# State products on half tiles of the array with one query plane, and the inverse of the running decays as one wide reciprocal in place of a backward scan

## The chip, the cores and the metric

The kernel runs on one core of one Trainium2 chip. The metric is the device time of one execution in microseconds (us). The core has a matrix engine (TensorE, PE in the profile, with its weight loads as PEld), three engines for elementwise work (VectorE or DVE, ScalarE or ACT, GpSimd or POOL), and SyncE (SP), which issues the transfers. Each engine works through its own instructions in order.

## The reference

A gated linear attention, followed by two feed-forward layers:

```python
# B, H, S, D = 4, 8, 768, 48; one 48 x 48 state for each batch and head
for t in range(S):
    state = alpha[:, :, t, :, None] * state + np.einsum('bhd,bhe->bhde', k[:, :, t], v[:, :, t])
    y[:, :, t] = np.einsum('bhd,bhde->bhe', q[:, :, t], state)
x = y.transpose(0, 2, 1, 3).reshape(3072, 384)
h = x @ w_in                      # 384 x 2048
x = (h * np.cos(h)) @ w_out       # 2048 x 384
out = ((x @ w_a) * (x @ w_b)) @ w_out2   # 384 x 1536, 1536 x 384
```

All arrays are float32, and alpha lies between 0.8 and 1.

## The kernel before

**The attention** is cut into 48 units: unit u is one batch and one chunk of 64 steps, with its 8 heads laid out as 4 pairs. The even head of a pair stands on partitions 64 to 111, the odd one on 0 to 47 (`HEADS`). For each unit the kernel does the following.

- *Front* (`plan_front`). DVE scans the running product of the decays `a` (L303, 112 x 260: 4 pairs of 65 columns, column 0 of each is 1). It then needs the inverse `r = 1/a`: a reciprocal of the last column of each pair (L312, 112 x 4, into `last`), and a scan from the right (L315, 112 x 260) that multiplies this by the decays step by step. POOL writes `m = q * a` (L327, for each head of the pair an instruction of its own, 48 x 256), and `k * r` is made by DVE for the first eight units and by POOL for the others (L340). ACT sums the squares of `a` and `r` (L344); this sum decides at the end whether the numbers were in range.
- *Scores* (`plan_scores`). PE multiplies the scaled keys with the scaled queries (L374) and transposes the keys (L383); ACT copies the transposed keys to SBUF (L389, `kn`), and DVE masks the scores into plane 0 of `m` (L407, or L413 from unit 16 on).
- *Back* (`plan_back`). PE makes the new state (L444, and L450 to add the old one) and the outputs: scores times values (L461), and, for units below `APART` = 16 that have a predecessor, the old state `s` times the scaled queries (L466). There are 14 such units. In L466 a product has 112 rows: the tile `m` has three planes, and planes 1 and 2 hold the queries of one head each, with zeros on the rows of the other head. ACT and DVE move the outputs to the tile `x_t` (L505, L508), and DVE multiplies the new state by the last decay (L535).

From unit 16 on the state is put beside the values, so that L461 alone makes the outputs.

**The layers.** A step of layer 1 is a block of 9 matrix products on `hp` (L656), then round, fraction, sine, product and a split in two parts that ACT and DVE take in turns (L706, L709, L714, L717, L721, L725), then 9 products into `acc_t` (L663). There are 96 such steps. Sixteen weight tiles for it are decoded on the way (ACT L599, L604 and L625, DVE L610 and L616, POOL L636), from transfers into `st_t`. Layer 2 follows.

**What sets the order.** `Plan` is a list scheduler that runs when the kernel is built. Each operation has an engine, a planned time in us, what it comes after, and at times a due time; the order that it finds is what each engine gets. An operation with `port=True` is not planned beside another one with that flag, be it on DVE or on POOL. The planned times are numbers in the code: 0.18 for the reciprocal L312 and 0.7 for the scan L315.

Of the kernel before, what the change touches and what calls it, by code (L numbers as in the profile page):

```python
# [10 lines left out]
F32 = mybir.dt.float32  # L11
# [6 lines left out]
ALU = mybir.AluOpType  # L18

B, H, S, D = 4, 8, 768, 48  # L20
# [4 lines left out]
C = 64  # L25
NCH = S // C
NU = B * NCH
NP = H // 2
P = 128
KT = DM // P  # L30
# [9 lines left out]
NE4 = NP * D  # L40
# [16 lines left out]
APART = 16  # L57
NLATE = NPAIR2 - NPAIR1
DVE_DECAY = 0
ACT_LOW = 16  # L60
# [106 lines left out]
def chunked(ctx: ExitStack, tc: tile.TileContext, u_in: bass.AP, wts: bass.AP, out: bass.AP, in_range: bass.AP):  # L167
# [18 lines left out]
    first = att.tile([112, NP, SEP], F32, name="first", bufs=1)  # L186
    last = att.tile([112, NP, SEP], F32, name="last", bufs=1)
    nc.vector.memset(first, 0.0)
    nc.vector.memset(last, 0.0)
    nc.vector.memset(first[:, :, 0:1], 1.0)  # L190
    mask = att.tile([P, 1, 1, C], F32, name="mask", bufs=1)
    nc.gpsimd.memset(mask, 1.0)
    for r0 in (0, 64):
# [3 lines left out]
        )  # L197
    m_t = [att.tile([P, 3, NP, C], F32, name=f"m{i}", bufs=1) for i in range(3)]
    for i, t in enumerate(m_t):
        (nc.gpsimd if i else nc.vector).memset(t[:, 1:3], 0.0)  # L200
    s_t = [att.tile([112, NE4], F32, name=f"s{i}", bufs=1) for i in range(2)]
# [54 lines left out]
    def part(u, i):  # L256
        return un[u]["in"][0:112, NA + i * NC4:NA + (i + 1) * NC4].rearrange("p (c t) -> p c t", t=C)
# [16 lines left out]
    def plan_load(u):  # L274
        d, ops = un[u], U[u]
        if "ld" in ops:
            return ops["ld"]
        def load():
            if u < UG:
                t = wpool.tile([P, 2, 2 * DM], F32R, name="w_t").bitcast(F32)  # L280
                d["in"] = t.rearrange("p a c -> p (a c)")[:, 0:IN_COLS]
            else:
                d["in"] = att.tile([P, IN_COLS], F32, name="in_t", bufs=NIN)
            cols = W_A + 2 * NE4 if u < APART else IN_COLS
            cuts = (0, NA + 1, cols) if u == 0 else (0, cols)
            for c0, c1 in zip(cuts, cuts[1:]):
                nc.sync.dma_start(out=d["in"][:, c0:c1], in_=u_in[u, :, c0:c1])

        ops["ld"] = op(SP, 1.5, load, lag=1.7)
        ops["in_last"] = take("w_t", NPAIR1, ops["ld"]) if u < UG else take("in", NIN, ops["ld"])  # L290
        return ops["ld"]

    def plan_front(u):
# [17 lines left out]
        def recip():  # L311
            nc.vector.reciprocal(last[:, :, C:SEP], d["a"][:, :, C:SEP])  # L312

        def scan_r():
            nc.vector.tensor_tensor_scan(  # L315
                d["r"].rearrange("p c t -> p (c t)")[:, ::-1], d["in"][0:112, NA:0:-1],
                last.rearrange("p c t -> p (c t)")[:, ::-1], 0.0, op0=ALU.mult, op1=ALU.add,
            )

        rc = op(DVE, 0.18, recip, [sa, U[u - 1]["sr"] if u else None])  # L320
        sr = ops["sr"] = op(DVE, 0.7, scan_r, [rc], port=True)
        m = m_t[u % 3]
# [4 lines left out]
                lambda rows=rows, i=i: nc.gpsimd.tensor_tensor(  # L327
                    m[rows, i + apart], part(u, 0)[rows], d["a"][rows, :, 1:], op=ALU.mult
                ),
                [sa, *m_before], port=True,  # L330
            )
            for rows, i in HEADS
        ]
# [28 lines left out]
    def plan_scores(u, block=None):  # L362
# [7 lines left out]
        def score():  # L370
            for c in range(2):
                for b in range(2):
                    for rows, h in HEADS:
                        nc.tensor.matmul(  # L374
                            sc_t[rows_of(b, h), b, c, :], kt[rows, 2 * b + c, :],
                            m[rows, h + apart, 2 * b + c, :], start=True, stop=True,
                        )
# [44 lines left out]
    def plan_back(u):  # L422
# [32 lines left out]
        def outputs():  # L455
            for p in range(NP):
                b, c = divmod(p, 2)
                for h, r0, n in ((0, 0, C), (1, 64, D)):
                    w = d["in"][:, W_A + h * NE4 + p * D:W_A + h * NE4 + p * D + n]
                    k_rows = P if apart or h else 112  # L460
                    nc.tensor.matmul(  # L461
                        ys_t[r0:r0 + n, b, c, :], w[0:k_rows], m[0:k_rows, 0 if apart else h, p, :],
                        start=True, stop=not carry,
                    )
                    if carry:
                        nc.tensor.matmul(  # L466
                            ys_t[r0:r0 + D, b, c, :], s_t[u % 2][:, p * D:p * D + D], m[0:112, h + 1, p, :],
                            start=False, stop=True,
                        )
            if u < UG:  # L470
                keep_warm(1)
# [10 lines left out]
        else:  # L482
# [10 lines left out]

            us = ou = op(PE, 1.75 + (1.0 if carry else 0.0), block, [kn, ld, *mk, *ma, *before], due=due)
        ops["us_op"] = [us]
# [439 lines left out]
def step_by_step(  # L935
# [76 lines left out]
    with tc.For_i(0, NG, 1) as g:  # L1012
        cols = bass.ds(g * G, G)
        x = pool.tile([P, KT, G], F32, name="g_x", bufs=1)
        for j in range(KT):
            for r0, f0, n in (
                (0, 2 * j * D, D), (48, 6 * D + j, 16), (64, (2 * j + 1) * D, D), (112, 7 * D + j, 16)
            ):
                step = KT if n == 16 else 1
                nc.sync.dma_start(out=x[r0:r0 + n, j, :], in_=y_all[f0:f0 + (n - 1) * step + 1:step, cols])  # L1020
# [115 lines left out]
```

## Time and profile before

| | us |
|---|---|
| median of 3 runs (lowest, highest) | 976.39 (975.45, 978.84) |
| profiled execution | 973.26 |
| its span in the trace | 971.4 |
| PE busy in the span | 939.9 |
| DVE busy | 540.5 |
| ACT busy | 403.2 |
| POOL busy | 226.5 |

The span of the trace is 1.9 us shorter than the profiled execution's own time. The page cuts the span into 40 slices of 24.3 us and shows a tenth of busy time with each digit; the attention fills the first 18 slices, beside layer 1. A windows table gives the same in us for stretches that one chooses. In a timeline the first number is the start, the second the duration, and brackets give the idle time of the engine before the instruction and what ended it.

### The profile page before, as it was taken

How to read it: one execution, taken by the hardware profiler on the slowest of the kernel's cores; microseconds unless marked ns; L12 is line 12 of the kernel's file. 1: busy time of each engine (PE TensorE's matmuls, PEld its weight loads, DVE VectorE, ACT ScalarE, POOL GpSimd, SP SyncE). 2: the span in 40 equal slices, each digit the busy share in tenths (PEclk: the TensorE clock that was granted, in tenths of full speed). 3: DMA queues.
4: the chain of work that ended last, by engine and by line, in shares of the span. 5: the costliest groups of instructions: out<-in, count | busy, mean ns of one | idle time of the engine just before them, and what ended most of it. 6: DMA issues, size and time to landing. Idle time of an engine off the chain costs nothing.

```text
span 971.4 us, 16849 instructions
## 1 busy us (share of the span) xinstructions
PE 939.9 (97%) x6935; PEld 766.3 (79%) x6935; DVE 540.5 (56%) x951; ACT 403.2 (42%) x754; POOL 226.5 (23%) x259
## 2 busy tenths in 40 slices
PE   6798989999999999999999999999999999999996
PEld 4677768888888888888887888888888888888884
DVE  7899998767777786776777842222222222222221
ACT  3477755545545455446665523112113113112111
POOL 4556543313322232312224321001001001000000
PEclk8999999999999999999999999999999999999998
DMA  9355412212221221203223400000000000000000
GB/s 369 106 199 184 164 38 78 90 62 81 88 63 54 89 89 54 64 1 139 98 98 112 149 0 33 1 1 33 1 0 33 1 1 33 0 1 33 1 1 36
DMA packets 17700, 64.96 MB, mean 67 GB/s; under 512 B 2384, under 2 KB 4816, under 8 KB 17616
## 3 DMA queue, kind: packets, MB, share of 16 engines
q1 hardware_dynamic: 17616, 63.81, 19.0%
q8 instruction: 56, 0.92, 0.4%
q14 instruction: 28, 0.23, 0.1%
HBM read 56.72 MB, written 4.72 MB: 63 GB/s over the span
## 4 chain that ended last, share of the span: by engine, by line
PE 87%; DVE 6%; DMA 2%; ACT 2%; issue 1%; POOL 1%; SPq 0%; ACTq 0%
PE acc_t L663 33%; PE hp L656 18%; PE xy L656 15%; PE ap L656 15%; PE xy L461 2%; DMA st_t<-wts 2%; PE xy L374 1%; DVE wf_t L610 1%; DVE wf_t L616 1%; DMA w_t<-u_in 1%; PE xy L383 1%; DVE c_t L709 1%; DVE ar_t L303 1%; PE xy L444 1%; DVE glo_t L725 1%
## 5 line engine op out<-in xcount | busy, mean ns | idle before, releaser
L663 PE MATMUL acc_t<-ghi_t,w_t 128*128 128x512 f32 x972 | 301.1, 391 | 1.0 <-ACT ghi_t L721 1.0
L656 PE MATMUL hp<-x_t,w_t 128*128 128x512 f32 (+1 forms) x882 | 216.4, 390 | 3.2 <-DMA x_t<-x_t 3.2
L663 PEld LDWEIGHTS acc_t<-ghi_t,w_t 128*128 128x128 f32 x972 | 181.6, 188 | 39.3 <-ACT ghi_t L721 1.9
L663 PE MATMUL acc_t<-glo_t,w_t 128*128 128x512 f32 x486 | 190.1, 391 | 3.8 <-DVE glo_t L725 3.8
L822 DVE TENSOR_TENSOR xy<-c_t,xy 128x512 f32<-128x512 f32 x72 | 50.1, 696 | 258.0 <-PE xy L656 257.9
L656 PEld LDWEIGHTS hp<-x_t,w_t 128*128 128x128 f32 x882 | 161.1, 188 | 36.8 <-ACT w_t L625 3.3
L656 PE MATMUL xy<-x_t,w_t 128*128 128x512 f32 x594 | 145.6, 390 | 0.0
L656 PE MATMUL ap<-x_t,w_t 128*128 128x512 f32 x540 | 132.2, 389 | 0.0
L656 PEld LDWEIGHTS xy<-x_t,w_t 128*128 128x128 f32 x594 | 111.5, 188 | 23.4
L656 PEld LDWEIGHTS ap<-x_t,w_t 128*128 128x128 f32 x540 | 101.4, 188 | 21.1
L819 ACT COPY c_t<-ap 128x512 f32<-128x512 f32 x72 | 42.3, 587 | 167.9 <-PE ap L656 167.8
L663 PEld LDWEIGHTS acc_t<-glo_t,w_t 128*128 128x128 f32 x486 | 91.2, 188 | 25.6 <-DVE glo_t L725 6.4
L826 ACT CAST ghi_t<-xy 128x512 fp32r<-128x512 f32 x72 | 42.2, 586 | 138.3 <-DVE xy L822 138.3
L706 ACT ACTIVATE c_t<-hp 128x512 int32<-128x512 f32 x96 | 57.5, 599 | 67.4 <-PE hp L656 67.1
L636 POOL TENSOR_TENSOR w_t<-wf_t,w_t 128x768 fp32r<-128x768 f32 x32 | 64.0, 1999 | 92.1 <-ACT w_t L625 92.1
L781 POOL TENSOR_TENSOR x_t<-x,x_t 128x512 fp32r<-128x512 f32 x18 | 23.7, 1343 | 251.0 <-ACT x_t L778 251.0
L714 ACT ACTIVATE c_t<-c_t 128x512 f32<-128x512 f32 x96 | 60.6, 631 | 46.7 <-DVE c_t L709 45.9
L709 DVE CUSTOM_DVE_ANT_0 c_t<-c_t,hp 128x512 f32<-128x512 int32 x96 | 65.6, 683 | 25.6 <-ACT c_t L706 24.7
L721 ACT CAST ghi_t<-hp 128x512 fp32r<-128x512 f32 x96 | 56.4, 587 | 54.1 <-DVE hp L717 53.5
L717 DVE TENSOR_TENSOR hp<-c_t,hp 128x512 f32<-128x512 f32 x96 | 65.8, 685 | 19.7 <-ACT c_t L714 19.2
L830 DVE TENSOR_TENSOR glo_t<-xy,ghi_t 128x512 fp32r<-128x512 f32 x72 | 49.8, 692 | 47.3 <-ACT ghi_t L826 47.3
L725 DVE TENSOR_TENSOR glo_t<-hp,ghi_t 128x512 fp32r<-128x512 f32 x96 | 65.7, 684 | 17.1 <-ACT ghi_t L721 16.3
(100 smaller groups left out, 923.3 us busy)
## 6 DMA issues: line engine op xcount, KB each, us to landing
st_t<-wts SPq DMA_DIRECT2D x34, 768.0 KB, 4.3
in_t<-u_in SPq DMA_DIRECT2D x32, 626.0 KB, 3.8
in_t<-u_in SPq DMA_DIRECT2D x8, 578.0 KB, 9.5
out<-o_t SPq DMA_DIRECT2D x18, 256.0 KB, 2.1
w_t<-u_in SPq DMA_DIRECT2D x7, 578.0 KB, 7.8
x_t<-x_t SPq DMA_DIRECT2D x48, 48.0 KB, 2.9
w_t<-u_in SPq DMA_DIRECT2D x1, 447.5 KB, 3.5
w_t<-u_in SPq DMA_DIRECT2D x1, 130.5 KB, 2.2
```

What stands on the lines that cost most here:

```text
L636: nc.gpsimd.tensor_tensor(t[:, 1], conv.pop(i), t[:, 0].bitcast(F32), op=ALU.subtract)
L656: nc.tensor.matmul(acc, wt[:, w, j * P:(j + 1) * P], r[:, j, :], start=i == 0, stop=i == len(terms) - 1)
L663: nc.tensor.matmul(accs[j], wt[:, w, j * P:(j + 1) * P], r, start=first and i == 0, stop=last and i == 2)
L706: nc.scalar.activation(s["c"].bitcast(I32), s["u"], AF.Identity, bias=-0.25, scale=-1.0)
L709: nc.vector._custom_dve(TENSOR_ADD_SAT, out=s["c"], in0=s["c"].bitcast(I32), in1=s["u"], s0=0.25, s1=-0.75)
L714: nc.scalar.activation(s["c"], s["c"], AF.Sin, bias=math.pi / 2, scale=TWO_PI)
L717: nc.vector.tensor_tensor(s["u"], s["c"], s["u"], op=ALU.mult)
L721: nc.scalar.copy(s["hi"], s["u"])
L725: nc.vector.tensor_tensor(s["lo"], s["u"], s["hi"].bitcast(F32), op=ALU.subtract)
L819: nc.scalar.copy(s["c"], s["a"])
L822: nc.vector.tensor_tensor(s["b"], s["c"], s["b"], op=ALU.mult)
L830: nc.vector.tensor_tensor(s["lo"], s["b"], s["hi"].bitcast(F32), op=ALU.subtract)
```

## The change

- `r` is now one reciprocal of all of `a`, 112 x 260 (planned time 0.42, no `port`). The backward scan, the tile `last` and its clearing are gone.
- `m` has two planes for all units. For units below 16 plane 1 holds the queries of both heads, written by one POOL instruction of 112 x 256 where there were two of 48 x 256. The clearing of planes 1 and 2 (one instruction on DVE, two on POOL) is gone.
- The product of the old state with the queries takes 48 rows for each head, at partitions 64 and 0, and writes to either half of the output's partitions. The eight of them stand behind the eight products of scores and values, not between them.
- For this the two heads of the second bank (pairs 2 and 3) change places in the outputs, so the rows of `w_in` and the slices of the fallback path are permuted (`LOW`, `HIGH`).
- A load for a unit below 16 has 16 more columns, 1172 for 1156.
- The planned time of a block of PE work from unit 8 on is 1.5 us, and 0.85 more with an old state (1.75 and 1.0 before).

```diff
+LOW, HIGH = (0, 2, 5, 7), (1, 3, 4, 6)
...
-    last = att.tile([112, NP, SEP], F32, name="last", bufs=1)
     nc.vector.memset(first, 0.0)
-    nc.vector.memset(last, 0.0)
...
-    m_t = [att.tile([P, 3, NP, C], F32, name=f"m{i}", bufs=1) for i in range(3)]
-    for i, t in enumerate(m_t):
-        (nc.gpsimd if i else nc.vector).memset(t[:, 1:3], 0.0)
+    m_t = [att.tile([P, 2, NP, C], F32, name=f"m{i}", bufs=1) for i in range(3)]
...
-            cols = W_A + 2 * NE4 if u < APART else IN_COLS
+            cols = W_A + 2 * NE4 + C - D if u < APART else IN_COLS
...
         def recip():
-            nc.vector.reciprocal(last[:, :, C:SEP], d["a"][:, :, C:SEP])
-
-        def scan_r():
-            nc.vector.tensor_tensor_scan(
-                d["r"].rearrange("p c t -> p (c t)")[:, ::-1], d["in"][0:112, NA:0:-1],
-                last.rearrange("p c t -> p (c t)")[:, ::-1], 0.0, op0=ALU.mult, op1=ALU.add,
-            )
-
-        rc = op(DVE, 0.18, recip, [sa, U[u - 1]["sr"] if u else None])
-        sr = ops["sr"] = op(DVE, 0.7, scan_r, [rc], port=True)
+            nc.vector.reciprocal(d["r"], d["a"])
+
+        sr = op(DVE, 0.42, recip, [sa])
...
-                    m[rows, i + apart], part(u, 0)[rows], d["a"][rows, :, 1:], op=ALU.mult
+                    m[rows, i], part(u, 0)[rows], d["a"][rows, :, 1:], op=ALU.mult
...
-            for rows, i in HEADS
+            for rows, i in (((slice(0, 112), 1),) if apart else HEADS)
...
-                            m[rows, h + apart, 2 * b + c, :], start=True, stop=True,
+                            m[rows, 1 if apart else h, 2 * b + c, :], start=True, stop=True,
...
-                for h, r0, n in ((0, 0, C), (1, 64, D)):
+                for h in range(2):
+                    rows = rows_of(b, h)
+                    n = D if rows.start else C
...
-                        ys_t[r0:r0 + n, b, c, :], w[0:k_rows], m[0:k_rows, 0 if apart else h, p, :],
-                        start=True, stop=not carry,
+                        ys_t[rows.start:rows.start + n, b, c, :], w[0:k_rows], m[0:k_rows, 0 if apart else h, p, :],
+                        start=not carry or c == 0, stop=not carry,
                     )
-                    if carry:
-                        nc.tensor.matmul(
-                            ys_t[r0:r0 + D, b, c, :], s_t[u % 2][:, p * D:p * D + D], m[0:112, h + 1, p, :],
-                            start=False, stop=True,
-                        )
+            if carry:
+                for c in range(2):
+                    for b in range(2):
+                        for rows, h in HEADS:
+                            p, r0 = 2 * b + c, rows_of(b, h).start
+                            nc.tensor.matmul(
+                                ys_t[r0:r0 + D, b, c, :], s_t[u % 2][rows, p * D:p * D + D], m[rows, 1, p, :],
+                                start=False, stop=c == 1,
+                            )
...
-            us = ou = op(PE, 1.75 + (1.0 if carry else 0.0), block, [kn, ld, *mk, *ma, *before], due=due)
+            us = ou = op(PE, 1.5 + (0.85 if carry else 0.0), block, [kn, ld, *mk, *ma, *before], due=due)
```

The new planned times move rows on all engines. Three places follow. The line numbers are those of each kernel: L300, L309, L330, L397, L504 and L531 after are L303, L312, L340, L407, L508 and L535 before; L334, L379, L501, L595 and L600 are L344, L389, L505, L599 and L604; L440, L453 and L462 are L450, L461 and L466.

DVE, units 1 to 3, before. `ar_t` holds `a` and `r`, `s` is the state carried on, `xy` and `acc_t` are the PSUM tiles of alternate units:

```order
L303 SCALAR_TENSOR_TENSOR ar_t<-w_t,first 112x260
L312 RECIPROCAL last<-ar_t 112x4
L315 SCALAR_TENSOR_TENSOR ar_t<-w_t,last 112x260
L340 TENSOR_TENSOR k_108<-ar_t,w_t 112x256
L303 SCALAR_TENSOR_TENSOR ar_t<-w_t,first 112x260
L407 TENSOR_TENSOR m_99<-xy,mask 128x256
L312 RECIPROCAL last<-ar_t 112x4
L315 SCALAR_TENSOR_TENSOR ar_t<-w_t,last 112x260
L340 TENSOR_TENSOR k_107<-ar_t,w_t 112x256
L303 SCALAR_TENSOR_TENSOR ar_t<-w_t,first 112x260
```

And after, from the same scan of unit 1 on:

```order
L300 SCALAR_TENSOR_TENSOR ar_t<-w_t,first 112x260
L309 RECIPROCAL ar_t<-ar_t 112x260
L397 TENSOR_TENSOR m_97<-xy,mask 128x256
L330 TENSOR_TENSOR k_103<-ar_t,w_t 112x256
L300 SCALAR_TENSOR_TENSOR ar_t<-w_t,first 112x260
L309 RECIPROCAL ar_t<-ar_t 112x260
L531 TENSOR_TENSOR s_101<-xy,ar_t 112x192
L397 TENSOR_TENSOR m_98<-acc_t,mask 128x256
L330 TENSOR_TENSOR k_102<-ar_t,w_t 112x256
L504 SCALAR_TENSOR_TENSOR x_t<-xy,x_t 112x4x64
```

The wide reciprocal stands where the narrow one and the backward scan stood, ahead of the mask of the unit in front and of the keys of its own.

ACT, units 1 to 3, before. L599 and L604 are the first work on a weight tile and need its transfer, L505 moves the outputs of a unit, L389 copies its transposed keys:

```order
L389 COPY kn_110<-acc_t 128x4x48
L344 ACTIVATE w_t,ranges<-ar_t 112x520
L599 ACTIVATE wf_t<-st_t 128x768
L505 ACTIVATE x_t<-acc_t 112x4x64
L389 COPY kn_109<-xy 128x4x48
L604 ACTIVATE st_t<-st_t 128x768
```

And after:

```order
L379 COPY kn_105<-acc_t 128x4x48
L334 ACTIVATE w_t,ranges<-ar_t 112x520
L501 ACTIVATE x_t<-acc_t 112x4x64
L379 COPY kn_104<-xy 128x4x48
L334 ACTIVATE w_t,ranges<-ar_t 112x520
L501 ACTIVATE x_t<-xy 112x4x64
L379 COPY kn_105<-acc_t 128x4x48
L595 ACTIVATE wf_t<-st_t 128x768
L600 ACTIVATE st_t<-st_t 128x768
```

The first work on a weight tile moved from ahead of unit 1's outputs to behind unit 2's outputs and unit 3's keys.

PE, the end of unit 1's block, before (the pattern goes on for 16 rows), `s_106` being the old state:

```order
L450 MATMUL acc_t<-s_106,ident 112x96 x2
L461 MATMUL acc_t<-m_100,w_t 64x64
L466 MATMUL acc_t<-m_100,s_106 48x64
L461 MATMUL acc_t<-m_100,w_t 48x64
L466 MATMUL acc_t<-m_100,s_106 48x64
L461 MATMUL acc_t<-m_100,w_t 64x64
L466 MATMUL acc_t<-m_100,s_106 48x64
```

And after:

```order
L440 MATMUL acc_t<-s_101,ident 112x96 x2
L453 MATMUL acc_t<-m_98,w_t 64x64
L453 MATMUL acc_t<-m_98,w_t 48x64
L453 MATMUL acc_t<-m_98,w_t 64x64
L453 MATMUL acc_t<-m_98,w_t 48x64 x2
L453 MATMUL acc_t<-m_98,w_t 64x64
L453 MATMUL acc_t<-m_98,w_t 48x64
L453 MATMUL acc_t<-m_98,w_t 64x64
L462 MATMUL acc_t<-m_98,s_101 48x64 x8
```

The products with the old state moved from between the others to behind them, and the 48-column products of pairs 1 and 2 now follow each other.

## Rows read from the trace of the kernel before

**Rows 1.** The page: busy tenths of three engines in 40 slices

```profile
PE   6798989999999999999999999999999999999996
DVE  7899998767777786776777842222222222222221
PEclk8999999999999999999999999999999999999998
```

**Rows 2.** Windows: stretch, length, busy time (instructions) by engine, clock, DMA

```profile
0.00:40.00 40.00, 29.91 (x657) 22.35 (x659) 29.14 (x66) 17.90 (x41) 18.12 (x33) 0.91 0.68 263
40.00:133.50 93.50, 81.77 (x945) 65.45 (x942) 88.43 (x128) 65.86 (x119) 56.92 (x42) 0.98 0.47 162
133.50:440.00 306.50, 306.50 (x3048) 248.47 (x3049) 231.42 (x496) 154.56 (x322) 91.67 (x150) 1.00 0.20 65
140.00:200.00 60.00, 60.00 (x648) 48.54 (x647) 48.83 (x108) 31.77 (x70) 21.61 (x35) 1.00 0.25 80
```

**Rows 3.** The chain that ended last, 130 to 142 us: start, length, what

```profile
130.94 0.60 DVE hp L717
131.54 0.59 DVE c_t L709
...
132.74 0.70 DVE glo_t L725
...
133.48 1.88 PE acc_t L663 x7
135.37 2.05 PE hp L656 x9
```

**Rows 4.** Groups on DVE up to 133.5 us: count, busy us, mean ns

```profile
L315 DVE TENSOR_TENSOR_SCAN ar_t<-in_t,last 112x260 f32<-112x260 f32 x9 | 6.9, 762 | 0.0
L315 DVE TENSOR_TENSOR_SCAN ar_t<-w_t,last 112x260 f32<-112x260 f32 x8 | 6.2, 776 | 0.3
L312 DVE RECIPROCAL last<-ar_t 112x4 f32<-112x4 f32 x18 | 3.1, 173 | 0.2
```

**Rows 5.** Groups on DVE, whole span: small and plain operations

```profile
L902 DVE TENSOR_SCALAR good<-total 112x1 f32<-112x1 f32 x1 | 0.2, 153 | 0.0
L901 DVE TENSOR_REDUCE total<-ranges 112x1 f32<-112x48 f32 x1 | 0.2, 196 | 0.0
L407 DVE TENSOR_TENSOR m<-xy,mask 128x256 f32<-128x256 f32 x12 | 4.9, 407 | 0.0
```

**Rows 6.** By line: duration ns as min/median/max

```profile
L312 DVE RECIPROCAL last<-ar_t x48: 165/174/183, 3.8 to 410.8; 112x4 f32<-112x4 f32 x48
L340 DVE TENSOR_TENSOR k<-ar_t,w_t x8: 415/426/728, 4.8 to 31.8; 112x256 f32<-112x256 f32 x8
```

**Rows 7.** Timeline of DVE and ACT in the first 20 us

```profile
3.08 0.70 DVE L303 TENSOR_TENSOR_SCAN ar_t<-w_t,first 112x260 f32<-112x260 f32 x1 [0.76 <-DMA w_t<-u_in]
...
19.41 0.43 DVE L340 TENSOR_TENSOR k<-ar_t,w_t 112x256 f32<-112x256 f32 x1 [3.16 <-PE xy L383]
...
18.62 0.90 ACT L599 ACTIVATE wf_t<-st_t 128x768 f32<-128x768 f32 x1 [5.53 <-DMA st_t<-wts]
19.43 0.36 ACT L505 ACTIVATE x_t<-acc_t 112x256 fp32r<-112x256 f32 x1
```

**Rows 8.** Timeline, 44 to 50 us: a scan beside POOL

```profile
44.49 1.39 POOL L327 TENSOR_TENSOR m<-in_t,ar_t 48x256 f32<-48x256 f32 x1
45.27 3.00 DVE L303 TENSOR_TENSOR_SCAN ar_t<-in_t,first 112x260 f32<-112x260 f32 x1
45.85 1.86 POOL L636 TENSOR_TENSOR w_t<-wf_t,w_t 128x768 fp32r<-128x768 f32 x1
```

**Rows 9.** Timeline of PE: unit 15's block, then the first without an old state

```profile
118.83 0.33 PE L461 MATMUL xy<-m,in_t 128*64 128x64 f32 x4
...
119.94 0.46 PE L374 MATMUL xy<-m,k 48*64 48x64 f32 x16
120.22 0.40 PE L383 MATMUL xy<-ident,k 48*64 48x48 f32 x16
...
141.43 0.68 PE L461 MATMUL xy<-m,in_t 112*64 112x64 f32 x16
142.04 0.46 PE L374 MATMUL xy<-m,k 48*64 48x64 f32 x16
```

**Rows 10.** Groups on POOL: the queries' products and the keys'

```profile
L327 POOL TENSOR_TENSOR m<-in_t,ar_t 48x256 f32<-48x256 f32 x80 | 60.0, 750 | 37.0 <-DVE ar_t L303 32.3 <-DVE last L312 1.5
L340 POOL TENSOR_TENSOR k<-ar_t,in_t 112x256 f32<-112x256 f32 x40 | 32.6, 815 | 166.5 <-PE xy L383 99.0 <-DVE ar_t L315 33.9 <-PE xy L444 17.4
```

More of the change, by code (lines that the diff above doesn't have):

```diff
@@ L1016, in step_by_step @@
             for r0, f0, n in (
-                (0, 2 * j * D, D), (48, 6 * D + j, 16), (64, (2 * j + 1) * D, D), (112, 7 * D + j, 16)
+                (0, LOW[j] * D, D), (48, LOW[3] * D + j, 16), (64, HIGH[j] * D, D), (112, HIGH[3] * D + j, 16)
             ):
@@ L1107 @@
     perm = np.stack([
-        np.concatenate([rows[2 * j], rows[6, j::KT], rows[2 * j + 1], rows[7, j::KT]])
+        np.concatenate([rows[LOW[j]], rows[LOW[3], j::KT], rows[HIGH[j]], rows[HIGH[3], j::KT]])
         for j in range(KT)
```

## The prediction

> **What bounds the kernel now.** I read the page's 40 slices first, then windows by stage, then the chain of waits, then groups and a timeline where a term needs one. In the slices [rows 1] PE shows 9 from the seventh on, but 6 to 9 ahead of that, while DVE shows 9 in slices 3 to 6. The windows [rows 2] say it in us. In 0 to 40 us no engine is full: DVE 29.1, PE 29.9. In the 93.5 us after that DVE is busy for 88.4 and PE for 81.8. From 133.5 to 440 us PE is busy for all of 306.5 us, and DVE for 231.4. The chain [rows 3] changes hands at the same place: up to 133.4 us its pieces are DVE's, and from 133.48 us on they are PE's blocks, end to end. So there are two stages. **Before 133.5 us** a us of DVE work moves the end unless one of DVE's idle spells takes it; a us that PE saves there is worth little. **After 133.5 us** a us of PE work moves the end, and DVE has 75 us free. What the first stage loses is not won back, since PE is full behind it.
>
> [...]
>
> **The change, part by part.**
>
> *The wide reciprocal.* Up to 133.5 us there are 18 narrow reciprocals of 173 ns and 17 backward scans of 762 to 776 ns, together 0.94 us for each unit [rows 4]. In their place stands a reciprocal of 260 columns, which the trace does not show, so its price needs bounds. The narrow one, 4 columns, takes 174 ns at the median [rows 6]. A plain operation on one column takes 153 ns [rows 5]: 21 ns for 3 more columns, or 7 ns a column. The sum over 48 columns gives the same: a plain operation costs about 1.0 ns a column (407 ns at 256 columns less 153 at one [rows 5], 254/255), so 196 - 48 leaves 148 ns without columns, and (174 - 148)/4 = 6.5 ns. With 7 ns the wide one takes 174 + 256 x 7 = 1.97 us. From below: if the extra 21 ns are a fixed part of this operation, the columns go at the plain rate, and the nearest row is the product of 256 columns, 0.42 us [rows 6]. In between, the shortest narrow one, 165 ns, gives 4 ns a column and 1.2 us; from above, the longest, 183 ns, gives 10 ns and 2.7 us. I take 1.97, because the row it is worked out from is the operation itself: a plain operation on 4 columns should take 156 ns, and none of the 48 takes less than 165. Per unit that is 1.97 - 0.94 = +1.03 us, and for 18 units **+18.5 us** of DVE work ahead of the hand-over (from 0.42: -9.4; from 2.7: +31.7).
>
> [...]
>
> *What covers it.* DVE is idle for 10.9 of the first 40 us and for 5.1 of the next 93.5 [rows 2]. The first 1.7 us lie ahead of the first scan, at 3.08 us [rows 7], and cover nothing. The largest spell, 3.16 us ahead of the keys of unit 3 at 19.41 us, goes back to ACT, which stood 5.53 us before L599 for a weight transfer with unit 1's outputs (L505) queued behind it [rows 7]. In the new order L599 stands behind two more units' outputs and keys, so this spell goes, and DVE works in it. Of the other spells in the first stretch I count half, some 3 us. In the second I count 2 us. Two-source operations of DVE also stand beside POOL's: a scan takes 0.70 us alone and 3.00 with POOL's L327 and L636 beside it [rows 7, 8]. The wide reciprocal is planned without the port flag, POOL can get through while it runs, and POOL has less to do (below); I count 2 us. In all 3.2 + 3 + 2 + 2 = 10 us of 18.5 are covered, and **+8.5 us** remain. If no cover holds it is +18.5; if all of the idle time and some of the stalls cover it, about 0.
>
> *POOL.* Sixteen units have one product of 112 x 256 where two of 48 x 256 stood, 750 ns each. The keys' product has the new shape and takes 815 [rows 10]. So POOL saves some 0.7 us a unit, 11 us in all; it is off the chain but for the stalls above, in which I have counted it. The three memsets that go lie ahead of 3.08 us, where DVE waits for its first load: nothing.
>
> *State products on half tiles.* In unit 15 the block of outputs with an old state takes 119.94 - 118.83 = 1.11 us; without one, 142.04 - 141.43 = 0.61 [rows 9]. So the eight state products cost 0.50. Half-tile products of the new shape are in the trace: the eight scores take 120.22 - 119.94 = 0.28 us. That saves 0.22 us in each of 14 units, 3.1 us of PE work. All 14 end by 119.9 us, in the stage in which PE has 11.7 us to spare [rows 2]. Where the outputs lie in the loop from unit to unit (units 2 to 7) they could give 6 x 0.22 = 1.3 us, but with the wide reciprocal DVE is the later one there. I take 0, and -1.3 as the bound.
>
> *The order of the outputs.* In all units two 48-column products now follow each other on the same half of the output's partitions. In units 16 to 47 that lies on the full PE. The 16 instructions of such a block take 0.61 us, 38 ns each; if one of them can't overlap with its neighbour, that is 38 ns x 32 units = 1.2 us, if it makes no difference 0. I take **+0.5**.
>
> *After the hand-over.* Thirty units are still to come, which puts 30 us on DVE's 231.4 of 306.5. The tightest stretch is 140 to 200 us, with 7 units: 48.8 + 7 x 1.03 = 56 of 60 us [rows 2]. It fits, but with little room, and what DVE makes late PE waits for. I take **+1** and a bound of +5. Loads grow by 16 of 1156 columns, with the DMA engines at 0.2 to 0.7 of their time: nothing.
>
> **The sum.** 8.5 + 0.5 + 1 = +10 us on the profiled execution's 973.3, so 983.3. The median of the runs is 3.1 us above that execution, and the forecast is for the median: 976.4 + 10 = **986.4 us**.
>
> **The rivals.**
>
> 1. *The columns go at the plain rate.* Then a unit saves 0.94 - 0.42 = 0.52 us of DVE. Nine units lie in the second stretch, where DVE is full: 4.7 us. In the first, ACT's wait no longer holds up the units (3.2 us), and the shorter fronts and blocks add about 1. **967.4 us**, faster. For it: the planned time is the plain rate, and 21 ns is little to work from. Against it: no narrow reciprocal comes near 156 ns, so the operation differs from a plain one in some way already at 4 columns. This decides as soon as the wide reciprocal is under 0.94 us.
>
> 2. *A slow reciprocal that is covered.* At 4 ns a column it takes 1.2 us, 0.26 more than what it replaces: 18 x 0.26 = 4.7 us, less than the cover. The moved ACT rows then give back a little more than the rest costs: **975 us**, within the measurement's reach. The same comes of 1.97 us if all idle time covers. For it: the idle time is there, 16 us in all. Against it: most of the spells in the first 40 us are waits in the loop through PE and ACT, which stay.
>
> 3. *PE is held after the hand-over too.* At 2.7 us a unit DVE has 48.8 + 7 x 1.76 = 61 us of work in the 60 from 140 to 200 us, and PE, full until now, waits. With 31.7 - 10 us ahead of the hand-over and about 5 behind, it ends near **1003 us**.
>
> **How the numbers follow.** A measurement of this kernel can tell about 0.3% (3 us) from no change. Forecast, 978 to 1000 us: 0.57. Rival 1: 0.25, of which 0.02 lie within 3 us. Rival 2: 0.13, of which 0.03 are faster and 0.02 slower by more than 3 us. Rival 3: 0.05. Faster is then 0.26, no change 0.11 (with 0.01 of the forecast's lower edge), slower 0.63. The range has to hold 8 in 10. The forecast's own, 978 to 1000, comes from the reciprocal between 1.5 and 2.5 us and the cover between 5 and 14; it holds not much over half, so the range goes down over rival 2 and into rival 1, to 964, which leaves out rival 3 and the lower end of rival 1.
>
> **What would show it.** The row of the wide reciprocal, 1.97 us against 0.42, settles most. If the forecast holds, DVE is over 95% busy from about 10 us to the hand-over, the 5.53 us wait of ACT is gone, the chain passes from DVE to PE about 8 us later, and PE is then busy to within a few us as long as before. The state products take 0.28 us in a block. I am wrong if the wide reciprocal is short; if the hand-over moves by much less than DVE's added work, so that the idle spells covered more; or if PE shows waits on DVE behind the hand-over.

## The result, and the profile after

The kernel after takes 989.81 us (987.70 to 990.99), the kernel before, run beside it, 975.92 (975.30 to 978.84): a ratio of 1.0134, 95% interval 1.0107 to 1.0161, or **13.9 us more** where 10 more were forecast. The profiled execution took 990.99 us; its span is 989.2, which is 17.8 more than the 971.4 of the profiled execution before: that pair lies further apart than the medians. Two of the ten runs of g3_scan_warm below (998.12 and 1005.08 us) were in a slower state and are left out of its row.

The page of after, the rows that answer to [rows 1]:

```profile
PE   7888899999999999999999999999999999999996
DVE  5699998888787887876778852222222222222221
PEclk7579999999999999999999999999999999999998
```

Windows of after over the stretches of [rows 2] (stretch, length, busy us and instructions of PE, PEld, DVE, ACT, POOL, then granted clock, DMA share, GB/s):

```profile
0.00:40.00 40.00, 30.42 (x469) 21.44 (x470) 26.25 (x42) 14.12 (x32) 6.51 (x18) 0.62 0.64 245
40.00:133.50 93.50, 82.77 (x1001) 65.91 (x1001) 85.82 (x113) 60.66 (x111) 41.39 (x33) 0.87 0.47 162
133.50:440.00 306.50, 302.46 (x3040) 244.52 (x3040) 256.45 (x460) 155.68 (x327) 99.30 (x151) 0.99 0.21 67
140.00:200.00 60.00, 58.09 (x594) 46.16 (x593) 53.75 (x96) 30.99 (x66) 23.07 (x34) 1.00 0.18 61
```

The row to look at is the first. With a longer operation in every unit, DVE is busy for *less* of the first 40 us than before (26.25 us for 29.14), and PE has done 469 instructions for 657 in the same busy time. PE's side of that stands in the clock: 0.62 of the full clock for 0.91, and a 5 in the second slice of the page, half of the full clock.

The chain of waits of after, at the place of [rows 3]:

```profile
146.97 0.70 DVE glo_t L721
147.68 0.04 issue
147.72 1.89 PE acc_t L659 x7
```

It passes from DVE to PE at 147.72 us, 14.2 later than at 133.48. So 14.2 of the 17.8 us between the two spans are lost by then. From the hand-over to the end of the span it is 841.5 us for 837.9, 3.6 more. Three of PE's waits between 140 and 560 us, which before doesn't have, add up to about that (engine, tile and line, what it waited for: us in all, times, longest):

```profile
PE xy L453 <- DVE m L403: 2.1, 1, 2.1
PE acc_t L659 <- ACT ghi_t L717: 1.1, 1, 1.1
PE acc_t L659 <- DVE glo_t L721: 0.6, 2, 0.3
```

The wide reciprocal by its line (durations in ns, shortest, median, longest):

```profile
L309 DVE RECIPROCAL ar_t<-ar_t x48: 1762/1775/1779, 3.7 to 433.0; 112x260 f32<-112x260 f32 x48
```

PE of after, the block of unit 1 with its eight state products (L462), and a later one:

```profile
16.82 0.68 PE L462 MATMUL acc_t<-m,s 48*48 48x64 f32 x16
17.43 0.63 PE L667 MATMUL acc_t<-zeros 128*64 128x512 bf16 x1
...
54.90 2.29 PE L652 MATMUL hp<-x_t,w_t 128*128 128x256 f32 x9
...
60.20 0.44 PE L462 MATMUL xy<-m,s 48*48 48x64 f32 x16
60.46 0.41 PE L364 MATMUL xy<-m,k 48*64 48x64 f32 x16
```

The state products take 17.43 - 16.82 = 0.61 us at a granted clock of 0.50 (window of 16 to 18 us), and 60.46 - 60.20 = 0.26 at 1.00 (60 to 61 us). The first block of layer 1 starts at 54.90 us; before it starts at 37.63.

DVE of after, the masks (L397) of units 2 to 4 and what stands between them:

```profile
19.56 0.43 DVE L397 TENSOR_TENSOR m<-xy,mask 128x256 f32<-128x256 f32 x1 [0.69 <-ACT kn L379]
...
23.96 0.42 DVE L504 SCALAR_TENSOR_TENSOR x_t<-acc_t,x_t 112x256 fp32r<-112x256 f32 x1 [3.65 <-PE acc_t L667]
24.30 0.69 DVE L300 TENSOR_TENSOR_SCAN ar_t<-w_t,first 112x260 f32<-112x260 f32 x1
25.03 1.78 DVE L309 RECIPROCAL ar_t<-ar_t 112x260 f32<-112x260 f32 x1
...
26.93 0.41 DVE L397 TENSOR_TENSOR m<-acc_t,mask 128x256 f32<-128x256 f32 x1
...
32.78 0.43 DVE L397 TENSOR_TENSOR m<-xy,mask 128x256 f32<-128x256 f32 x1 [0.69 <-ACT kn L379]
```

This is a loop in which the engines take turns. DVE stands 3.65 us until PE has done a block; then a scan and a reciprocal stand ahead of the next mask in DVE's queue, and PE waits for that mask. The masks of the first eight units start at 9.68 and 49.48 us in after, 5.7 us apart on average, and at 9.70 and 38.16 in before, 4.1 apart. Before, they come in pairs: two units are in the loop at a time. After, they come one by one. The masks of units 3 to 6 before:

```profile
24.00 0.42 DVE L407 TENSOR_TENSOR m<-acc_t,mask 128x256 f32<-128x256 f32 x1
25.28 0.40 DVE L407 TENSOR_TENSOR m<-xy,mask 128x256 f32<-128x256 f32 x1
31.49 0.42 DVE L407 TENSOR_TENSOR m<-acc_t,mask 128x256 f32<-128x256 f32 x1
33.03 0.42 DVE L407 TENSOR_TENSOR m<-xy,mask 128x256 f32<-128x256 f32 x1
```

DVE was idle for 10.9 of the first 40 us before. These are its two largest waits behind 10 us, in the form of the table above:

```profile
DVE s L535 <- ACT x_t L505: 3.7, 5, 1.1
DVE k L340 <- PE xy L383: 3.2, 1, 3.2
```

The first of them is five waits in the same loop, which runs through PE and ACT; the second goes back to ACT's wait for a weight transfer [rows 7]. In after DVE is idle for 13.75 of the first 40 us.

### The profile page after: what moved, and what is told of

Read it like the earlier page. It is cut to its first block, busy times and chain, and to the rows that moved or that the text cites. A ratio compares the mean times of both kernels' runs of the same rounds, so it can differ in the third digit from the quotient of the medians.

```text
span 989.2 us, 16781 instructions
## 1 busy us (share of the span) xinstructions
PE 955.6 (97%) x6935; PEld 776.7 (79%) x6935; DVE 571.8 (58%) x901; ACT 403.2 (41%) x754; POOL 208.6 (21%) x241
## 3 DMA queue, kind: packets, MB, share of 16 engines
q1 hardware_dynamic: 17616, 63.94, 18.6%
## 4 chain that ended last, share of the span: by engine, by line
PE 84%; DVE 8%; DMA 3%; issue 2%; ACT 1%; POOL 0%; SPq 0%; ACTq 0%
PE acc_t L659 31%; PE hp L652 16%; PE xy L652 15%; PE ap L652 15%; PE xy L453 2%; DMA in_t<-u_in 2%; PE xy L364 1%; DMA st_t<-wts 1%; DVE ar_t L309 1%; DVE wf_t L606 1%; DVE ar_t L300 1%; DVE wf_t L612 1%; DVE c_t L705 1%; DVE hp L713 1%; DVE glo_t L721 1%
## 5 line engine op out<-in xcount | busy, mean ns | idle before, releaser
L652 PE MATMUL hp<-x_t,w_t 128*128 128x512 f32 (+1 forms) x882 | 218.9, 394 | 0.0
L652 PEld LDWEIGHTS hp<-x_t,w_t 128*128 128x128 f32 x882 | 164.2, 192 | 34.2 <-issue 0.4
L309 DVE RECIPROCAL ar_t<-ar_t 112x260 f32<-112x260 f32 x48 | 85.1, 1774 | 0.8
L632 POOL TENSOR_TENSOR w_t<-wf_t,w_t 128x768 fp32r<-128x768 f32 x32 | 63.3, 1978 | 94.8 <-ACT w_t L621 94.8
```

The lines of the kernel that those rows point to most:

```text
L309: nc.vector.reciprocal(d["r"], d["a"])
L632: nc.gpsimd.tensor_tensor(t[:, 1], conv.pop(i), t[:, 0].bitcast(F32), op=ALU.subtract)
L652: nc.tensor.matmul(acc, wt[:, w, j * P:(j + 1) * P], r[:, j, :], start=i == 0, stop=i == len(terms) - 1)
```

## The experiments

Each was run beside the kernel before, which took 975.2 to 976.0 us at the median. The three columns in the middle are read in the windows and the timeline of one profiled execution of each kernel: the granted clock in three stretches, and where the first block of layer 1 starts.

| kernel | us (lowest, highest) | ratio (95%) | clock in 20-30, 30-40, 40-50 us | layer 1 from |
|---|---|---|---|---|
| before | | | 1.00, 1.00, 0.84 | 37.6 |
| after | 989.81 (987.70, 990.99) | 1.0107-1.0161 | 0.50, 0.50, 0.50 | 54.9 |
| e1_scan_back | 984.02 (976.34, 989.21) | 1.0035-1.0118 | 0.50, 0.50, 0.50 | 53.1 |
| e2_recip_only | 998.01 (995.04, 1000.31) | 1.0191-1.0263 | 0.84, 0.50, 0.84 | 47.8 |
| e3_true_cost | 987.65 (986.26, 989.03) | 1.0106-1.0166 | 0.50, 0.50, 0.50 | 56.2 |
| e4_warm | 990.40 (984.97, 995.10) | 1.0104-1.0211 | 0.82, 0.50, 0.50 | 55.7 |
| f1_times | 974.38 (971.22, 976.76) | 0.9965-0.9995 | 0.83, 1.00, 0.79 | 38.3 |
| f2_behind | 974.55 (970.50, 977.71) | 0.9966-1.0003 | 0.77, 1.00, 0.75 | 38.6 |
| f4_no_fill | 977.35 (973.54, 978.90) | 1.0004-1.0031 | 1.00, 1.00, 0.66 | 36.3 |
| g1_48rows | 982.06 (980.36, 983.09) | 1.0035-1.0080 | 0.50, 0.50, 0.55 | 45.8 |
| g2_112rows | 975.67 (971.28, 977.42) | 0.9979-1.0012 | 1.00, 1.00, 0.83 | 37.9 |
| g3_scan_warm | 982.85 (977.58, 987.78) | 1.0040-1.0088 | 1.00, 1.00, 0.57 | 50.0 |
| g4_recip_planned | 986.72 (983.96, 987.99) | 1.0087-1.0137 | 0.76, 0.58, 0.84 | 51.5 |
| h1_recip_from_8 | 971.78 (971.00, 975.38) | 0.9949-0.9986 | 0.99, 1.00, 0.88 | 38.4 |

### Each half alone: e1_scan_back, e2_recip_only

After with the backward scan put back:

```diff
...
-            nc.vector.reciprocal(d["r"], d["a"])
-        sr = op(DVE, 0.42, recip, [sa])
+            nc.vector.reciprocal(last[:, :, C:SEP], d["a"][:, :, C:SEP])
+        def scan_r():
...
+        rc = op(DVE, 0.18, recip, [sa, U[u - 1]["sr"] if u else None])
+        sr = ops["sr"] = op(DVE, 0.7, scan_r, [rc], port=True)
```

> The changed kernel with the backward scan in place of the wide reciprocal; half-tile state products, one query plane and planned times of PE blocks as in the changed kernel. Theory 1 (the wide reciprocal's 1.77 us on VectorE, 0.83 us more per unit than what it replaced, makes the 14 us): the loss goes, 972 to 977 us, hand-over from DVE to PE at 129 to 134 us. [...]

Two more theories were tried here and in e2, e3 and e4. By theory 2 the clock of 0.50 from 10 to 57 us makes most of the loss and comes with the reciprocal: without it the loss goes too, and the clock is back at 1.00 by about 25 us. By theory 3 it comes with the half-tile state products: the clock stays at 0.50 to beyond 40 us, and the time is 981 to 988 us.

And before with nothing but the wide reciprocal, planned at 0.42 us as in after (the same lines with the signs turned).

> The kernel before with nothing but the wide reciprocal in place of the narrow one and the backward scan. Theory 1: 987 to 993 us, whatever the clock does. [...]

By theory 2 the time was to be the same, with the clock at 0.50 to beyond 40 us; by theory 3 the clock was to be back by 25 us and the time to be 979 to 985 us.

Without any wide reciprocal 8 us are lost, and PE is granted a clock of 0.50 from 20 to 60 us (e1). So the reciprocal isn't needed for the low clock, and a theory by which its DVE work makes all of the 13.9 us falls. The other number was a miss: in e2 the reciprocal alone costs 22 us, more than the whole change and more than any of the three theories gave it.

### The plan's number: e3_true_cost, g4_recip_planned

e3 is after with one number changed, the planned time of the reciprocal:

```diff
-        sr = op(DVE, 0.42, recip, [sa])
+        sr = op(DVE, 1.75, recip, [sa])
```

> The changed kernel with 1.75 us in place of 0.42 as the planned time of the wide reciprocal: the same work in another order. Theory 1: DVE's work ahead of the hand-over is the same, so within 4 us of the changed kernel (986 to 994). [...]

By theory 2 the time was to fall to 980 to 985 us where the clock comes back by 25 us.

g4 is e2 with that number, and with the planned times of PE's blocks as in after:

```diff
-        sr = op(DVE, 0.42, recip, [sa])
+        sr = op(DVE, 1.75, recip, [sa])
-            us = ou = op(PE, 1.75 + (1.0 if carry else 0.0), block, [kn, ld, *mk, *ma, *before], due=due)
+            us = ou = op(PE, 1.5 + (0.85 if carry else 0.0), block, [kn, ld, *mk, *ma, *before], due=due)
```

> The kernel before with the wide reciprocal, as in e2_recip_only (998.0 us), but planned at 1.75 us in place of 0.42, and with the PE blocks planned at 1.5 and 0.85 us as after. State products of 112 rows, interleaved, as before. If the 10 us that e2_recip_only lost behind the hand-over come from a plan that counts on a fast reciprocal, PE is full again from 160 us on, the hand-over stays 10 to 13 us later than before, and the time is 985 to 990 us. If they come from DVE's work itself, PE still waits there and the time is 995 to 1000 us.

In after the number makes no difference that can be told (1.0136 and 1.0134). In the kernel with the reciprocal alone the two numbers make 11.3 us, 998.01 to 986.72. The windows from 160 to 440 us show where, of e2 and then of g4:

```profile
160.00:440.00 280.00, 272.24 (x2697) 218.19 (x2693) 226.01 (x404) 132.48 (x282) 80.92 (x133) 0.98 0.22 69
...
```

```profile
160.00:440.00 280.00, 280.00 (x2805) 226.81 (x2806) 235.72 (x429) 141.25 (x298) 85.28 (x139) 1.00 0.22 68
```

With e2's plan PE is idle for 7.8 of 280 us behind the hand-over, with g4's for none. Most of those waits are for DVE's masks of the late units (L404, 5.7 us in three waits) and for `glo_t` (1.4 in two). In g4 the hand-over comes at 144.06 us, 10.6 later than before, as expected. Which of the two numbers does it wasn't tried apart. For the change, g4 is the comparison to use: **the wide reciprocal alone costs 11.0 us** against before (12.4 against f1 below, each beside its own runs of before; f1 has the same planned times of PE's blocks), and with it in place the half tiles (e3, the same planned numbers) add less than 1, which is within both intervals.

### What takes the clock: f1_times, f2_behind, g1_48rows, g2_112rows

Four things of the other half could do it: the new order that follows from the planned times, the state products behind the others, their 48 rows, and POOL's one product with the change of places of two heads. f1 is before with the block's planned times alone (the last two lines of the diff above).

> The kernel before with nothing but the new planned times of the PE blocks (1.5 and 0.85), so with the new order and the old work. [...]

If the products of 48 rows are what takes the clock in the first stage (theory A), the order alone does no harm: a clock of 1.00 again from about 20 us, layer 1 from near 38 us, 973 to 979 us. If the order does it (theory B), the clock stays at 0.50 to beyond 40 us and the time is 981 to 988 us.

f2 has in addition the state products behind the others, still with 112 rows and three planes of `m`:

```diff
-                        start=True, stop=not carry,
+                        start=not carry or c == 0, stop=not carry,
                     )
-                    if carry:
...
+            if carry:
+                for c in range(2):
+                    for b in range(2):
+                        p = 2 * b + c
+                        for h, r0 in ((0, 0), (1, 64)):
+                            nc.tensor.matmul(
+                                ys_t[r0:r0 + D, b, c, :], s_t[u % 2][:, p * D:p * D + D], m[0:112, h + 1, p, :],
+                                start=False, stop=c == 1,
+                            )
```

> The kernel before with the new planned times and the eight state products behind the eight products of scores and values, but of 112 rows and with three planes of m as before, and with the backward scan. [...]

Theory A gives the same clock and time here as for f1; theory B, and a theory C by which like products one behind the other keep the clock low, give 0.50 to beyond 40 us and 981 to 988 us.

Neither loses anything. That leaves the rows, the heads' places and POOL. g1 is e1 with three planes of `m` and POOL's two products, as before. Of its lines, the one of the state products:

```diff
...
-                                ys_t[r0:r0 + D, b, c, :], s_t[u % 2][rows, p * D:p * D + D], m[rows, 1, p, :],
+                                ys_t[r0:r0 + D, b, c, :], s_t[u % 2][rows, p * D:p * D + D], m[rows, h + 1, p, :],
```

> The kernel after with the backward scan, and with the three planes of m and the two query products of POOL for each unit as before: of the change there remain the state products of 48 rows behind the others, the change of places of two heads, and the planned times. [...]

By theory A the clock is 0.50 to beyond 40 us, layer 1 starts later than at 48 us, and the time is 981 to 988 us. If it is POOL's one product, which is ready earlier, the clock is 1.00 from about 25 us and the time 973 to 978 us.

And g2 is g1 with one line changed, by which each state product takes all 112 rows and meets zeros on the other head's:

```diff
-                                ys_t[r0:r0 + D, b, c, :], s_t[u % 2][rows, p * D:p * D + D], m[rows, h + 1, p, :],
+                                ys_t[r0:r0 + D, b, c, :], s_t[u % 2][:, p * D:p * D + D], m[0:112, h + 1, p, :],
```

> The same kernel as g1_48rows, but each of the eight state products takes all 112 rows, so that the rows of the other head meet zeros. Nothing else differs, neither order nor planned times nor POOL's work. [...]

By theory A the clock is 1.00 again from 20 to 25 us, layer 1 starts near 38 us and the time is 973 to 978 us, though the eight products take longer. If the places of the heads do it, g2 is as g1, with 981 to 988 us.

This pair settles it: 982.06 us with 48 rows, 975.67 with 112, same order, same plan, same POOL work, and the slowest of g2's ten runs (977.42) is faster than the fastest of g1's five (980.36). The product that does the job in less time makes the kernel **6.4 us slower**. PE of g1 in unit 1's block and the scores behind it, then the same of g2:

```profile
17.44 0.68 PE L473 MATMUL acc_t<-m,s 48*48 48x64 f32 x16
18.05 0.63 PE L678 MATMUL acc_t<-zeros 128*64 128x512 bf16 x1
18.61 0.71 PE L375 MATMUL xy<-m,k 48*64 48x64 f32 x16
19.09 0.62 PE L384 MATMUL xy<-ident,k 48*64 48x48 f32 x16
```

```profile
17.18 1.08 PE L473 MATMUL acc_t<-m,s 112*48 112x64 f32 x16
18.06 0.63 PE L678 MATMUL acc_t<-zeros 128*64 128x512 bf16 x1
18.62 0.65 PE L375 MATMUL xy<-m,k 48*64 48x64 f32 x16
19.10 0.39 PE L384 MATMUL xy<-ident,k 48*64 48x48 f32 x16
...
22.18 0.64 PE L473 MATMUL xy<-m,s 112*48 112x64 f32 x16
22.66 0.38 PE L678 MATMUL acc_t<-zeros 128*64 128x512 bf16 x1
```

The two run alike up to 18.6 us. In g2 the transposes behind the scores take 0.39 us, and the clock is 1.00 from 20 us on. In g1 they take 0.62, and the clock is 0.50 to 40 us and 0.55 from 40 to 50, though PE is busier than in g2 from 20 to 40 us (18.7 us for 16.5). Windows of g1, 20 to 40 us, then of g2:

```profile
20.00:30.00 10.00, 9.04 (x170) 7.40 (x170) 6.21 (x16) 6.21 (x14) 1.36 (x2) 0.50 0.61 245
30.00:40.00 10.00, 9.65 (x174) 7.51 (x170) 5.69 (x12) 2.86 (x8) 2.71 (x4) 0.50 0.08 22
```

```profile
20.00:30.00 10.00, 7.44 (x210) 6.17 (x212) 7.64 (x20) 7.22 (x17) 2.72 (x4) 1.00 0.61 243
30.00:40.00 10.00, 9.03 (x251) 7.57 (x246) 7.64 (x18) 5.08 (x12) 4.83 (x5) 1.00 0.31 102
```

At a clock of 0.50 PE becomes the bound of the first stage (9.65 of 10 us, DVE 5.69): of the chain of waits from 19 to 46 us, 22.1 of 27 us are PE's in g1 and 13.1 in g2. Layer 1 starts at 45.75 us for 37.91, earlier than the 48 that was expected. From its start to the hand-over both take about as long (95.4 us in g1, 94.5 in g2), so the loss arises in the first stage. What in the 48-row products keeps the clock down, the runs don't show; only that their rows do.

### What the clock is worth: f4_no_fill, e4_warm, g3_scan_warm

f4 is before without the one filling product on zeros (L671) behind each of the first eight units.

> The kernel before without the one filling product on zeros behind each of the first eight units. [...] If the clock comes back without it, the time is 973 to 978 us, and the run says nothing on the price of the clock.

If nothing but the granted clock separates the first stage of before from that with the half tiles, and the clock stays at 0.50 to beyond 40 us without the fill, layer 1 starts near 53 us and the time is 981 to 988 us.

The clock came back without it (1.00 from 20 to 40 us), so the run says nothing on the price. Two kernels add such products. e4 is after with two behind the scores of each of the first eight units, g3 is e1 with four. The line of g3:

```diff
...
-        ops["emit"] = [score] + ([transpose] if state else [])
+        ops["emit"] = [score] + ([transpose] if state else []) + ([lambda: keep_warm(4)] if u < UG else [])
```

> [...] Theory 1: no gain, 988 to 994 us, since DVE's work stays. [...]

By theory 2 the clock of e4 is back at 1.00 by about 25 us, layer 1 starts at 40 to 46 us, and the time is 977 to 984 us.

> [...] If the clock stays up and the time does not fall below 981 us, the lost 8 us are not the clock's. [...]

If the fill of g3 keeps the clock at 1.00 to 40 us and beyond and the clock is what was lost, layer 1 starts before 42 us and the time is 973 to 978 us; if the fill does not keep it up, the time is above 988 us.

In e4 the clock is 0.82 from 20 to 30 us and 0.50 behind that. In g3 it held at 1.00 to 40 us, layer 1 starts at 50.0 us, and the time did not change by more than the noise: 982.85 for 984.02. By the words on record, a clock that stays up with a time above 981 us says that the lost 8 us are not the clock's. That goes too far, since the fill is in the loop itself. It stands in one planned step with the scores, so the copies and the mask that wait for the scores can wait for the fill too, which takes 1.05 us a unit in g3's timeline. g3 also has the order of e1, masks one by one (17.57, 23.06, 28.18 us), some 5.3 us apart at the clock of 1.00, where the first eight masks of g2 with its pairs are 4.05 apart (10.09 to 38.44 us). So two handicaps of e1 are mixed here, the clock and the one-by-one order, and these two kernels don't take them apart. The clock's price rests on g1 and g2, where the order is the same. The six runs of e1, one program in one order, point the same way: the higher the granted clock over the span, the shorter the time, from 989.21 us at 0.964 to 976.34 at 0.981, with no run out of that order.

### Where the reciprocal costs: h1_recip_from_8

f1, with the wide reciprocal (planned at 1.75) from unit 8 on, and the scan for the first eight units:

```diff
-        rc = op(DVE, 0.18, recip, [sa, U[u - 1]["sr"] if u else None])
-        sr = ops["sr"] = op(DVE, 0.7, scan_r, [rc], port=True)
+        if u < UG:
+            rc = op(DVE, 0.18, recip, [sa, U[u - 1]["sr"] if u else None])
+            sr = ops["sr"] = op(DVE, 0.7, scan_r, [rc], port=True)
+        else:
+            sr = op(DVE, 1.75, lambda: nc.vector.reciprocal(d["r"], d["a"]), [sa])
```

> The kernel before with PE's blocks planned at 1.5 and 0.85, the backward scan kept for the first eight units, and the wide reciprocal (planned at 1.75) from unit 8 on. State products of 112 rows as before. The same kernel with the wide reciprocal in all units took 986.7 us. Theory W (what the reciprocal costs is DVE's work where DVE is full, from the first block of layer 1 to the hand-over): ten of the eighteen units ahead of the hand-over keep the longer step, 10 x 0.83 = 8.3 us less 2 us idle, so 980 to 984 us. [...]

Theory L stood against W: the loss arises in the first eight units, where the reciprocal stands in the loop from unit to unit and the clock is low for longer, and the stretch behind them makes room for it. By it layer 1 starts near 38 us, the clock is 1.00 from about 20 us, and the time is 974 to 978 us.

It takes 971.78 us, 0.9949 to 0.9986 of before; f1's interval overlaps with that. g4 differs from it in the first eight units' reciprocals alone (and in the order that their planned times give), and takes 986.72. Each beside its own runs of before, that is 11.0 us more and 3.4 less. So those eight cost 14.4 us, for 8 x (1.77 - 0.78 - 0.18) = 6.5 us of DVE work, and the other forty cost nothing that can be told. Where their work went is to be read from DVE's groups up to 134 us. f1 first (count, busy us, mean ns), then h1:

```profile
L616 DVE SCALAR_TENSOR_TENSOR wf_t<-st_t,wf_t 128x768 int32<-128x768 int32 x16 | 21.4, 1336 | 0.1
L610 DVE SCALAR_TENSOR_TENSOR wf_t<-wf_t,st_t 128x768 int32<-128x768 int32 x16 | 16.5, 1030 | 0.0
L303 DVE TENSOR_TENSOR_SCAN ar_t<-in_t,first 112x260 f32<-112x260 f32 x11 | 12.1, 1096 | 0.0
L315 DVE TENSOR_TENSOR_SCAN ar_t<-in_t,last 112x260 f32<-112x260 f32 x10 | 7.4, 740 | 0.0
```

```profile
L619 DVE SCALAR_TENSOR_TENSOR wf_t<-st_t,wf_t 128x768 int32<-128x768 int32 x16 | 19.7, 1232 | 0.1
L324 DVE RECIPROCAL ar_t<-ar_t 112x260 f32<-112x260 f32 x10 | 17.7, 1771 | 0.1
L613 DVE SCALAR_TENSOR_TENSOR wf_t<-wf_t,st_t 128x768 int32<-128x768 int32 x16 | 15.3, 958 | 0.0
L303 DVE TENSOR_TENSOR_SCAN ar_t<-in_t,first 112x260 f32<-112x260 f32 x10 | 8.9, 892 | 0.0
```

Ten reciprocals in place of ten scans and narrow reciprocals add 10 x (1771 - 740 - 175) = 8.6 us. The same decodes and scans beside them take 16 x 104 + 16 x 72 + 10 x 204 ns = 4.9 us less. By the windows of the two runs from 30 to 140 us, DVE is busy for 4.3 us more in h1, out of its idle time. Together that is 9.2 us for 8.6, and the hand-over is at 130.76 us for 131.99. The shorter scans and decodes would fit fewer stalls beside POOL, such as the scan of 3.00 us of [rows 8]: the reciprocal is planned without the port flag, so POOL's work can lie beside it and less of it beside the others. That was not tested by itself.

There is a second reading, and the chain of h1 from 38 to 134 us shows it. Four transfers of weights stand in it:

```profile
68.47 6.12 DMA st_t<-wts
80.23 6.12 DMA st_t<-wts
99.06 6.05 DMA st_t<-wts
111.26 5.93 DMA st_t<-wts
```

They are 24.2 of the 96 us; in f1 there are two such pieces (11.6 us), in before one (4.4). So DVE is over 90% busy in this stretch, but it is not what the end waits for all the time, and work of DVE that lies beside a transfer need not move the end. How much each of the two readings gives back was not tried apart.

## Why the prediction was right, and where it was not

The sign was right and the size near: +13.9 us, forecast +10, inside the forecast's own 978 to 1000. The way there was another, and that the number came out near is in part luck.

- *The wide reciprocal.* 1.775 us measured for the 1.97 taken, so 1.775 - 0.94 = 0.83 us a unit and 15.0 for 18 units, not 18.5. The 7 ns a column worked out from the narrow one was close: (1775 - 174) / 256 = 6.25. Rivals 1 and 2, which needed under 0.94 and about 1.2 us, fall with this row. Rival 2 in its other form, in which all idle time covers 1.97 us, falls with the hand-over, which came 14.2 us later.
- *The cover*, 10 us of it, is the step that failed, in both stretches and in opposite directions. In the first 40 us 6 us of DVE's idle time were counted as room. They are no room: apart from the 3.2 us that go back to ACT's weight transfer, DVE is idle there mostly in a loop through PE and ACT (3.7 us at L535), and 6.5 us of work put into the loop cost 14.4 (h1 against g4), with the change of order and clock that came with it. The spell of 3.16 us that was to go did go, but one of 3.65 us on PE stands in its place. In the 93 us behind that, where DVE is over 90% busy and 4 us were counted as cover, 8.6 us of work cost nothing, 4.9 by shorter neighbours and 4.3 out of idle time. The premise that a us of DVE work there moves the end is what failed; weight transfers stand in the chain too. The reciprocal alone costs 11.0 us, where 8.5 ahead of the hand-over was predicted: the two errors have opposite signs, and that they nearly cancel is luck.
- *The state products on half tiles.* The row was right (0.28 us predicted, 0.26 measured), and the value of 0 with a bound of -1.3 was wrong in sign: alone they cost 6.4 us (g1 against g2). What was missed is the clock: the prediction has no term for it in the first stage, though [rows 2] have the first 40 us at 0.91 and the page a clock of 8 in the first slice.
- *The terms don't add.* 11.0 and 6.4 would be 17.4; the change costs 13.9. Both act in the first eight units. With the reciprocal in it, the half tiles make no more difference that can be told (e3 against g4).
- *The order of the outputs*, +0.5: nothing that can be told. g2 has the new order and the change of places of the heads, and takes 975.67 us beside 975.69. A term of 0.5 is too small for these runs to show or to rule out.
- *POOL and ACT.* ACT's wait of 5.53 us at L599 is gone, as predicted: L595 starts at 25.95 us without one, and unit 1's outputs are moved at 18.10 us for 19.43. The loop behind that is slower by more.
- *After the hand-over*, +1 with a bound of 5: +3.6 in the two traces; the three waits above add up to 3.8 us. Rival 3, in which this makes much of the loss, is not what happened in after; it is what e2's plan gave, with a reciprocal of the same length.
- *What would show it.* DVE was to be over 95% busy from about 10 us to the hand-over. From 70 us on it nearly is (9.67 of the 10 us to 80, 58.6 of the 60 to 140); from 10 to 55 us it is busy for 29.6 of 45. That line is where the prediction's picture of the first stage is seen to be wrong. The hand-over was to come 8 us later, and came 14.2 later.

What stays open: how much of the 14.4 us of the first eight reciprocals is their own time in the loop, how much the order of one unit at a time, and how much the lower clock that g4 shows (0.76 and 0.58 from 20 to 40 us); and why 48 rows keep the clock down.

## What to carry to other kernels

Idle time of an engine inside a loop that passes from engine to engine is not room: ask what the added work stands in front of (6.5 us of DVE work cost 14.4 here). Where an engine is over 90% busy, on the other hand, follow the chain of waits before each us of added work is counted as lost: something else, such as a transfer, may set the pace in parts of the stretch (24.2 of 96 us in h1), and the engine's other operations may get shorter (by 4.9 us in h1). And where the granted clock is under 1.00 in a stretch of before (0.91 in the first 40 us here), a shorter matrix product can cost time there (6.4 us, g1 against g2); a change that costs nothing in the late units (h1) may have to be kept out of the first ones.

## What the runs showed of the hardware

- Eight products of 48 rows, the two heads of a pair on different rows, take 0.61 us at a granted clock of 0.50 (after, at 17 us) where eight of 112 rows take 18.06 - 17.18 = 0.88 (g2; the product on zeros behind takes 0.63 us in both); at a clock of 1.00 they take 0.26 (after, at 60 us) for 22.66 - 22.18 = 0.48 (g2).
- With the 48-row products (g1) PE was granted a clock of 0.50 from 20 to 40 us while busy for 18.7 of 20 us; with 112 rows (g2) it was granted 1.00 while busy for 16.5.
- The reciprocal of 112 x 260 takes 1.775 us, 6.25 ns for each column beyond the first four, 4.4 times the 407 ns of a plain operation on 256 columns. It keeps that time beside POOL's work (1.78 us at 97.81 us in after, with POOL's L632 from 97.52 to 99.44, 1.92 us for 1.87 at its median; all 48 lie between 1762 and 1779 ns), where a scan of the same columns went from 0.70 to 3.00 us [rows 7, 8].
